# A recurrent attention and its MLP on one core: from 128-token chunks with bf16 parts to 64-token chunks in 64 by 64 tiles of TensorE

## The chip, the cores and the metric

The kernel runs on one core of one Trainium2 chip. TensorE (PE) multiplies matrices into PSUM, VectorE (DVE), ScalarE (ACT) and GpSimd (POOL) work on tiles in SBUF, SyncE (SP) issues every DMA. The metric is the time of one execution on the device in microseconds, as the median of the timed runs.

## The reference

For 4 batches and 8 heads a recurrence runs over 768 tokens; its output, 320 wide per token, goes through an MLP of width 2048 with a hard-swish between the layers. The numbers of a step are 40 wide.

```python
for t in range(S):                       # S = 768, D = 40
    m_new = np.maximum(f_gate[:, :, t] + m, i_gate[:, :, t])
    f_stab = np.exp(f_gate[:, :, t] + m - m_new)
    i_stab = np.exp(i_gate[:, :, t] - m_new)
    m = m_new
    C = f_stab[:, :, None, None] * C + i_stab[:, :, None, None] * np.einsum('bhd,bhe->bhde', vt, kt)
    n = f_stab[:, :, None] * n + i_stab[:, :, None] * kt
    h_tilde = np.einsum('bhde,bhe->bhd', C, qt)
    nq = np.einsum('bhd,bhd->bh', n, qt)[:, :, None]
    denom = np.maximum(np.abs(nq), 1.0)
    o = 1.0 / (1.0 + np.exp(-o_gate[:, :, t]))
    y[:, :, t] = o * h_tilde / denom
h = x @ w_in                             # x: y as (3072, 320); w_in (320, 2048), w_out (2048, 320)
g = h * np.clip(h + 3.0, 0.0, 6.0) / 6.0
out = g @ w_out
```

## The kernel before

**Units and tasks.** The 3072 tokens are eight units `u` of 384 (half of a batch). A unit has two tasks of four heads each (`quad`), and a task three chunks of 128 tokens (`cp`), so there are 48 chunks with four heads. The attention of unit u+1 is computed beside the MLP of unit u; the attention of unit 0 stands alone at the start, and unit 7's MLP alone at the end.

**A chunk.** The recurrence is worked in chunks: `gates` makes running sums of the gates for all heads; `gate` builds the tile `gw` of decays between the tokens of a chunk (load of the sums by all partitions, causal select on POOL, line 637, four exponentials on ACT, line 642). `front` multiplies q by k (`s`), then DVE multiplies by `gw`. `state` adds the chunk's sum of k and v (`c`) to the decayed state C. `back` multiplies by v and adds what C gives (`o`); `fin` divides, gates, transposes (`xa`, `xb`) and splits the result into `xh` and `xl`. Column 40 of v is 1, so that n is a column of C; two columns pad it to 42 (`E2`).

**Precision.** TensorE's fp32 matmul appears as two records in a profile. The first tasks (`QT` = 3, `PT` = 4) use it. Later ones split q, k, v, C and p into three bf16 parts (`load_qk`, `split_v`, the end of `state`, `front`) whose products are summed; the parts of q, k and C are stacked in 120 rows by further DMAs (`st<-spl`, `cS<-d`).

**The MLP.** `mm1` makes one of 16 tiles `h` with eight matmuls of 384 columns, ACT and DVE make `g` of it and split it into `gh` and `gl`; `mm2` adds three products per pair into three banks `acc` (in unit 0 plain fp32, line 918). `weight_slice` decodes 16 slices of the weights through ACT, DVE and POOL into `whi`, `wlo`, `wtl` and `vr`, line 818.

**The order.** Nothing is scheduled by the compiler. Each helper above is a job that yields an engine and a cost; the class `Plan` places all jobs by due times, costs and free buffers, and the program is recorded in that order. On the chip every engine takes its own queue in that order, and waits where an operand isn't there. `warm` fills places in which the plan has TensorE idle before the MLP starts with dummy matmuls `pw`. The numbers at the top of the file (due times, costs, letters in `ENGINES` that choose an engine) are the plan's inputs.

[...]

Of the kernel before, what the change touches and what calls it, by code (L numbers as in the profile page):

```python
# [17 lines left out]
L = 128  # L18
# [7 lines left out]
E2 = D + 2  # L26
WS = 8
WC = 640
NEG = -1.0e30
BIG = 3.0e38  # L30
NATW = U * 4 * (D + E2)
W_TINY = 2.0
W_HUGE = 65536.0 * 122880.0 - 512.0
QT = 3
PT = 4
GB = 2
# [3 lines left out]
SPAN = 50.047  # L40
T0 = 52.817
AH = 22.494
GP = [1, 1, 4]
G0 = -68.728
G1 = 0.617
AH1 = 34.491
FC = 1
FCS = [[(0, 3)], [(0, 2), (2, 1)], [(0, 1), (1, 1), (2, 1)], [(0, 1), (1, 2)]]
LON = 0.423
WAI = 32.907  # L50
WAO = 3.016
WAS = -8.005
MV = -3.516
DELTA = -0.043
EGW = 1
EV = 34.901
EG = 9.989
# [7 lines left out]
RATE = 3500  # L65
WN = 128
DELTA0 = 0.305
# [3 lines left out]
BL = 5.478  # L71
T_WARM = 6.9
STX = {0: "st", 1: "st", 2: "st", 7: "st", 8: "st", 9: "st", 10: "qk", 11: "spl"}
WGAP = 0.055
ENGINES = 'dppdddxddaadddddxdaaaaadaax'
BG = -0.135
BA = -0.976
BD = 1.378
GS = 6
FD = 2  # L80
FIN0 = 8.437
# [205 lines left out]
def mlstm_moe_kernel(ctx: ExitStack, tc: tile.TileContext, ig, fg, qkd, natd, ond, w_in, w_out, ident_d, out):  # L287
# [19 lines left out]
    cT = cst.tile([128, NC, BH], F32, name="cT")  # L307
    eG = cst.tile([128, NC, BH], F32, name="eG")
    wT = cst.tile([128, NC, BH], F32, name="wT")
    dec = cst.tile([D, NC, BH], F32, name="dec")  # L310
    gsc = dram.tile([NC, BH, L], F32, name="gsc")
    nc.vector.memset(half, 0.5)

    plan = Plan(dict(wm=1, s=1, o=1, cx=1, es=2, eo=1, ecx=1, qk=1, nat=1, vp=1, spl=1, vb=2, st=3, gw=3, p=2, ht=2, d=2, on=1, x=2,
                     egw=EGW, y=NY, raw=NRAW, mm=2, acc0=1, acc1=1, acc2=1, g=2, gs=GS, ob=3))
# [10 lines left out]

    def banks(u, tag):
        return (tag, "e" + tag) if u == 0 else (tag,)
# [20 lines left out]
    def warm():  # L349
# [12 lines left out]
        f_s=[BH, S], i_s=[BH, S], m_s=[BH, S], lf=[BH, S], g_s=[BH, S], last=[128, 128], gTs=[128, NC, BH], mask=[128, L], one=[BH, L], sel=[BH, 4, L]).items()}  # L362
# [6 lines left out]
    def gates(c0, n):  # L369
        f_s, i_s, m_s, lf, g_s, last, gTs, mask, one = (GT[k] for k in ("f_s", "i_s", "m_s", "lf", "g_s", "last", "gTs", "mask", "one"))  # L370
        if c0 == 0:
            yield "q", 200, 0.95
            nc.sync.dma_start(f_s, fg)
            nc.sync.dma_start(i_s, ig)
            nc.vector.memset(one, 1.0)
            nc.vector.memset(lf[:, 0:1], 0.0)
            if GB:
                sel = GT["sel"]
                nc.gpsimd.memset(sel, 1.0)
                nc.gpsimd.affine_select(sel, sel, pattern=[[-1, 4], [0, L]], compare_op=ALU.is_equal, fill=0.0, base=0, channel_multiplier=1)  # L380
                nc.gpsimd.memset(mask, BIG)
                nc.gpsimd.affine_select(mask, mask, pattern=[[1, L]], compare_op=ALU.is_ge, fill=NEG, base=0, channel_multiplier=-1)
# [12 lines left out]
        nc.vector.tensor_sub(lf[:, b:z], lf[:, b:z], m_s[:, b:z])  # L395
        for c in cs:
            ks = slice(c * L, c * L + L)
            yield "d", ld(L)
            nc.vector.tensor_tensor_scan(g_s[:, ks], one, lf[:, ks], 0.0, ALU.mult, ALU.add)
            event(f"g_s{c}")  # L400
# [3 lines left out]
        nc.sync.dma_start(gsc[hs].rearrange("c r t -> r c t"), g_s[:, a:z].rearrange("p (c t) -> p c t", c=n))  # L404
# [6 lines left out]
        gs = yield ("get",) + banks(0, "s")  # L411
        pc = bank(gs, [128, n, BH], f"pc{c0}")
        yield "p", mat(n, 128, 1, 32, 32)
        for c in cs:
            nc.tensor.transpose(pc[:, c - c0, :], i_s[:, c * L : (c + 1) * L], ident[:BH, :BH])
        go = yield ("get",) + banks(0, "o")
        pg = bank(go, [128, n, BH], f"pg{c0}")
        yield "p", mat(n, 128, 1, 32, 32)
        for c in cs:
            nc.tensor.transpose(pg[:, c - c0, :], g_s[:, c * L : (c + 1) * L], ident[:BH, :BH])  # L420
# [641 lines left out]
```

## Time and profile before

| what | value |
|---|---|
| timed runs | 585.59, 587.58, 589.38 us, median 587.58 |
| profiled execution, first to last instruction | 591.0 us (its time is given by this span alone) |
| busy: PE, DVE, ACT, POOL | 91%, 68%, 57%, 24% of the span |
| granted clock of TensorE, mean | 0.913 |
| DMA | 69.26 MB, 117 GB/s |
| stores of the eight units begin at | 174.9, 233.1, 298.3, 366.4, 423.7, 483.7, 540.6, 586.0 us |

[...] An engine's idle time is put down to what ended it.

### The profile page before, as it was taken

The numbers are of one execution on the slowest core, as the hardware profiler recorded it, in microseconds if no ns is written. First come the engines' busy times: TensorE is split into PE (matmuls) and PEld (weight loads), VectorE is DVE, ScalarE is ACT, GpSimd is POOL, SyncE is SP. The second block draws the span as 40 slices with busy tenths as digits, with TensorE's granted clock in tenths as the row PEclk, the third lists the DMA queues.
The fourth block names the chain that finished last, engine by engine and source line by source line (L and its number), as shares of the span: only waits on it lengthen the run. The fifth ranks groups of instructions, "written<-read, shape, count | busy, mean of one in ns | idle before, by whom it ended". The sixth has DMA issues, their size and how long they took to land.

```text
span 591.0 us, 11413 instructions
## 1 busy us (share of the span) xinstructions
PE 540.3 (91%) x4207; PEld 493.6 (84%) x4207; DVE 404.1 (68%) x849; ACT 337.8 (57%) x738; POOL 141.0 (24%) x191
## 2 busy tenths in 40 slices
PE   8999999687799897999789997999978998999997
PEld 7988899476679797889678896999868997999997
DVE  6443476997588767779767775796957677685433
ACT  4521164474746756667666666676756567544433
POOL 3242111543530312221211322132212203110000
PEclk9555588788999999999889998999989999999999
DMA  8524137549316226253454135344534244300000
GB/s 280 145 74 154 41 109 192 159 149 259 123 48 180 96 77 180 83 145 97 140 178 143 37 112 158 105 136 139 155 112 144 67 123 140 123 15 34 1 1 34
DMA packets 34548, 69.26 MB, mean 117 GB/s; under 512 B 4301, under 2 KB 14725, under 8 KB 34493
## 3 DMA queue, kind: packets, MB, share of 16 engines
q1 hardware_dynamic: 34493, 68.54, 38.0%
q8 instruction: 33, 0.54, 0.4%
q14 instruction: 22, 0.18, 0.1%
HBM read 42.66 MB, written 4.03 MB: 79 GB/s over the span
## 4 chain that ended last, share of the span: by engine, by line
PE 57%; DMA 16%; DVE 12%; ACT 7%; SPq 3%; issue 2%; POOL 1%; DVEq 0%; POOLq 0%; ACTq 0%
PE h L877 20%; DMA gw<-gsc 6%; PE acc L920 5%; PE acc L922 5%; PE acc L921 5%; PE pw L359 3%; DMA nat<-in_nat_dram 3%; PE o L701 3%; PE s L659 2%; DMA qk<-in_qk_dram 2%; PE c L581 2%; PE o L708 2%; PE s L662 2%; DMA rawi<-in_w_in_dram 2%; PE acc L918 2%
## 5 line engine op out<-in xcount | busy, mean ns | idle before, releaser
L877 PE MATMUL h<-xh,whi 128*128 128x384 f32 x256 | 95.4, 373 | 17.9 <-DVE g L893 17.8
L893 DVE SCALAR_TENSOR_TENSOR g<-g,h 128x384 f32<-128x384 f32 x128 | 70.1, 551 | 60.3 <-ACT g L891 59.7
L920 PE MATMUL acc<-vh,gh 128*128 128x320 f32 x336 | 108.6, 323 | 1.4 <-ACT gh L339 1.4
L891 ACT ACTIVATE g<-h,half 128x384 f32<-128x384 f32 x128 | 73.6, 576 | 57.4 <-PE h L877 49.7
L922 PE MATMUL acc<-vh,gl 128*128 128x320 f32 x336 | 104.1, 310 | 0.1
L921 PE MATMUL acc<-vl,gh 128*128 128x320 f32 x336 | 104.1, 310 | 0.0
L877 PE MATMUL h<-xl,whi 128*128 128x384 f32 x256 | 88.7, 347 | 0.0
L877 PE MATMUL h<-xh,wlo 128*128 128x384 f32 x256 | 88.7, 346 | 0.0
L642 ACT ACTIVATE gw<-gw,cT 128x128 f32<-128x128 f32 x192 | 65.4, 393 | 32.9 <-POOL gw L637 32.8
L637 POOL TENSOR_SCALAR_AFFINE_SELECT gw<-gw 128x512 f32<-128x512 f32 x46 | 33.2, 722 | 187.8 <-DMA gw<-gsc 144.1
L901 DVE TENSOR_TENSOR gl<-g,gh 128x384 fp32r<-128x384 f32 x112 | 63.8, 573 | 19.0 <-ACT gh L339 18.3
L339 ACT CAST gh<-g 128x384 fp32r<-128x384 f32 x112 | 57.1, 511 | 30.3 <-DVE g L893 29.5
L877 PEld LDWEIGHTS h<-xh,whi 128*128 128x128 f32 x256 | 50.2, 196 | 24.0 <-DVE g L893 23.1
L920 PEld LDWEIGHTS acc<-vh,gh 128*128 128x128 f32 x336 | 63.6, 189 | 2.2 <-ACT gh L339 1.9
L922 PEld LDWEIGHTS acc<-vh,gl 128*128 128x128 f32 x336 | 63.4, 189 | 0.6 <-DVE gl L901 0.6
L921 PEld LDWEIGHTS acc<-vl,gh 128*128 128x128 f32 x336 | 63.7, 190 | 0.0
L339 ACT CAST p<-gw 128x512 bf16<-128x512 f32 x72 | 44.2, 614 | 19.7 <-DVE gw L666 13.8
L877 PEld LDWEIGHTS h<-xl,whi 128*128 128x128 f32 x256 | 50.3, 196 | 0.2
L877 PEld LDWEIGHTS h<-xh,wlo 128*128 128x128 f32 x256 | 50.2, 196 | 0.0
L877 PE MATMUL h<-xl,wtl 128*128 128x384 f32 x128 | 45.0, 352 | 0.4 <-DVE xl L784 0.3
L877 PE MATMUL h<-xh,wtl 128*128 128x384 f32 x128 | 44.5, 348 | 0.0
L666 DVE TENSOR_TENSOR gw<-s,gw 128x512 f32<-128x512 f32 x48 | 33.0, 687 | 16.7 <-PE s L662 9.5
(118 smaller groups left out, 1096.8 us busy)
## 6 DMA issues: line engine op xcount, KB each, us to landing
st<-spl SPq DMA_DIRECT2D x117, 160.0 KB
gw<-gsc SPq DMA_DIRECT2D x46, 256.0 KB
nat<-in_nat_dram SPq DMA_DIRECT2D x16, 492.0 KB
qk<-in_qk_dram SPq DMA_DIRECT2D x13, 480.0 KB
rawi<-in_w_in_dram SPq DMA_DIRECT2D x8, 640.0 KB
rawo<-in_w_out_dram SPq DMA_DIRECT2D x8, 640.0 KB
on<-in_on_dram SPq DMA_DIRECT2D x8, 480.0 KB
out_dram<-ob SPq DMA_DIRECT2D x24, 160.0 KB
```

Of the source, the lines that this page charges most:

```text
L339: nc.scalar.copy(dst, src)
L359: nc.tensor.matmul(pw[:, :WN], ones[:, :128], ones[:, :WN], start=True, stop=True)
L637: nc.gpsimd.affine_select(gw, gw, pattern=[[0, 4], [1, L]], compare_op=ALU.is_ge, fill=NEG, base=0, channel_multiplier=-1)
L642: nc.scalar.activation(gw[:, h, :], gw[:, h, :], AF.Exp, bias=cT[:, c, r0 + h : r0 + h + 1], scale=1.0)
L666: nc.vector.tensor_tensor(gw, sp, gw, ALU.mult)
L877: nc.tensor.matmul(hp, w, x, start=n == 0, stop=n == len(seq) - 1)
L891: nc.scalar.activation(g, hp, AF.Relu, bias=half, scale=1.0 / 6.0)
L893: nc.vector.scalar_tensor_tensor(g, g, 1.0, hp, ALU.min, ALU.mult)
L901: E(e).tensor_sub(gl, g, gh.bitcast(F32))
L920: nc.tensor.matmul(acc, gh[:, ts_], VH[f // 4][:, f % 4, :], start=f == 0, stop=False)
L921: nc.tensor.matmul(acc, gh[:, ts_], VL[p][:, f % 2, :], start=False, stop=False)
L922: nc.tensor.matmul(acc, gl[:, ts_], VH[f // 4][:, f % 4, :], start=False, stop=f == NF - 1)
```

## The change

Chunks are 64 tokens long, and two of them are worked together, so that a step still covers 128 tokens and four heads. Everything in attention is plain fp32; the bf16 parts, their casts and subtractions and their stacking DMAs are gone. The four 64 by 64 tiles of the array work on different heads or chunks: a matmul names its tile by the partitions of its operands (0 to 63 or 64 to 127) and of its output. One TensorE group writes one PSUM tile `xy` of two banks and holds B (the output) of the step before, S (q by k) and K (the state) of this one, 32 matmuls; in unit 0 S and K are one group and B another. `gate` works on 256 columns: the causal mask and the key's gate are added by DVE and one exponential follows. A task loads its gate sums at once. The state C is 128 partitions wide and steps twice per group. The heads of a unit are laid out in another order, and the rows of `w_in` with them. The cast for `vh` goes to DVE, the tail sums for `wtl` to POOL. The buffers are `st` 2, `nat` 2, `gw` 3 per task; before `nat`, `vp`, `qk` and `spl` had one each, `st` and `gw` three per chunk. The plan's inputs differ throughout; one line of them stands in the diff.

```diff
-ENGINES = 'dppdddxddaadddddxdaaaaadaax'
+ENGINES = 'dyxpxppdydaxdyyyzdaxxyadayydd'
-    plan = Plan(dict(wm=1, s=1, o=1, cx=1, es=2, eo=1, ecx=1, qk=1, nat=1, vp=1, spl=1, vb=2, st=3, gw=3, p=2, ht=2, d=2, on=1, x=2,
+    plan = Plan(dict(wm=1, xy=1, exy=1, z=1, es=1, eo=1, st=2, nat=2, gw=NGW, ht=2, on=1, x=2,
...
 def gate(task, cp):
...
+        else:
+            whole = task > 1
+            if not whole or cp == 0:
+                yield "wait", f"gsc{part * U + U - 1 if whole else c}"
+                lo, n = (part * U * L, U) if whole else (c * L, 1)
+                t0 = plan.now["t"]
+                for h in range(2):
+                    plan.now["t"] = t0
+                    yield "q", 66 * n
+                    r = 16 * h + 2 * bq
+                    nc.sync.dma_start((gt if whole else gw)[h * Q : h * Q + Q].rearrange("p j c t -> p j (c t)"), gsc[r : r + 2, lo : lo + n * L].partition_broadcast(Q))
+                event(f"gl{nm}")
+            elif whole:
+                yield "wait", f"gl{task}_0"
+            e = yield pick(27, g=0.72, d=ld(256))
+            E(e).tensor_tensor(gw, gw, mask[:, None, None, :].broadcast_to([128, 2, 2, Q]), ALU.add)
+        yield "wait", f"cT{c}"
+        e = yield pick(28, g=0.64, d=ld(256))
+        E(e).tensor_tensor(gw, gw, cT[:, 2 * c : 2 * c + 2, 2 * bq : 2 * bq + 2].rearrange("p c j -> p j c")[:, :, :, None].broadcast_to([128, 2, 2, Q]), ALU.add)
+        yield "a", ca(256) + 0.08
+        nc.scalar.activation(gw, gw, AF.Exp)
...
+    def group(g, parts):
+        u = parts[0][1] // (2 * U)
+        got = yield ("get", "xy", "exy") if u == 0 and g < GE else ("get", "xy")
+        pool = early["ps"] if got[0] == "exy" else ps_at
+        xy = pool.tile([128, 2, 512], F32, tag=f"{got[0]}{got[1]}", name=f"xy{g}")
...
+        for kind, n in parts:
+            task, cp = divmod(n, U)
...
+            if kind == "S":
+                st = T["st"][0]
+                for j in range(2):
+                    for c in range(2):
+                        rs = slice(c * Q, c * Q + D)
+                        for h in range(2):
+                            nc.tensor.matmul(xy[h * Q : h * Q + Q, c, j * Q : j * Q + Q], st[rs, cp, j, h], st[rs, cp, j, 2 + (h != c)], start=True, stop=True)
+            elif kind == "K":
+                for j in range(2):
+                    for c in range(2 if ch < NC - 1 else 1):
+                        rs = slice(c * Q, c * Q + Q)
+                        for h in range(2):
+                            o = (cp * 4 + 2 * h + j) * D
+                            nc.tensor.matmul(xy[h * Q : h * Q + KM, c, 296 + j * E2 : 296 + j * E2 + E2], T["kn"][rs, o : o + KM], T["vn"][rs, cp, 2 * h + j], start=True, stop=True)
+            else:
+                st, gt, vh = T["st"][0], T["gw"][0], T["vh"]
+                C0 = Cs.get((b, quad, ch - 1, 1), zero)
+                C1 = Cs[(b, quad, ch, 0)]
+                for j in range(2):
+                    for h in range(2):
+                        rs = slice(h * Q, h * Q + D)
+                        for c in range(2):
+                            nc.tensor.matmul(xy[c * Q : c * Q + Q, h, 212 + j * E2 : 212 + j * E2 + E2], st[rs, cp, j, 2 if c == h else 4], (C1 if c else C0)[rs, j], start=True, stop=True)
+                for j in range(2):
+                    for h in range(2):
+                        rs = slice(h * Q, h * Q + Q)
+                        for c in range(2):
+                            nc.tensor.matmul(xy[c * Q : c * Q + Q, h, 128 + j * E2 : 128 + j * E2 + E2], gt[rs, j, 2 * cp + c], vh[rs, cp, c, j], start=True, stop=True)
...
 def front(task, cp):
...
+        yield "d", cd(256)
+        nc.vector.tensor_tensor(gw, xy[:, :, 0:128].rearrange("p c (j t) -> p j c t", j=2), gw, ALU.mult)
...
 def state(task, cp):
...
+            Cn = at.tile([128, 2, E2], F32, tag=f"C{quad}", name=f"C{nm}_{c}", bufs=6)
+            if cur is None:
+                e = yield pick(8, a=ca(84), d=cd(84))
+                cast(e, Cn[:R], kv[:R, c])
+            else:
+                e = yield psub(16, 84)
+                E(e).tensor_tensor(Cn[:R], cur[:R], dec[:R, ch, c, 2 * bq : 2 * bq + 2, None].broadcast_to([R, 2, E2]), ALU.mult)
+                yield "d", cd(84)
+                nc.vector.tensor_add(Cn[:R], Cn[:R], kv[:R, c])
...
 def back(task, cp):
...
+        nc.vector.tensor_tensor(hv, xy[:, :, 212:296].rearrange("p h (j e) -> p h j e", j=2), heads(eG[:, c], bq)[:, :, :, None].broadcast_to([128, 2, 2, E2]), ALU.mult)
+        yield "d", cd(168)
+        nc.vector.tensor_add(hv, hv, xy[:, :, 128:212].rearrange("p h (j e) -> p h j e", j=2))
```

Three places of the order show the change. The first is TensorE in the middle of unit 2's MLP (`h2`): before, `c` of a chunk of task 7 stands there, followed by its `o`, of which the first matmuls are shown (`p`, `vb`, `st`, `cS` are bf16 parts).

```order
L877 MATMUL h2_11_3090<-xl2_1903,wtl_77 128x384
L581 MATMUL c7_1_3075<-vp7_2879,nat7_2841 40x42 x4
L703 LDWEIGHTS p7_1_2942
L703 MATMUL o7_1_3118<-vb7_2880,p7_1_2942 128x84
L704 LDWEIGHTS p7_1_2942
L704 MATMUL o7_1_3118<-vb7_2880,p7_1_2942 128x42
L705 LDWEIGHTS p7_1_2942
L705 MATMUL o7_1_3118<-vb7_2880,p7_1_2942 128x84
L706 LDWEIGHTS p7_1_2942
L706 MATMUL o7_1_3118<-vb7_2880,p7_1_2942 128x42
```

Now the last B of task 6 (`xy21`, by `st` and C, then by `gw` and `nat`) stands with S (`st` alone) and K of the first step of task 7 behind a piece of `h2`; the next piece of `h2` follows.

```order
L826 MATMUL h2_1_2746<-xl2_2092,wtl_77 128x384
L626 MATMUL xy21_2698<-C6_1_1_2620,st6_2063 64x42
L626 MATMUL xy21_2698<-C6_2_0_2677,st6_2063 64x42
L626 MATMUL xy21_2698<-C6_1_1_2620,st6_2063 64x42
L626 MATMUL xy21_2698<-C6_2_0_2677,st6_2063 64x42
L626 MATMUL xy21_2698<-C6_1_1_2620,st6_2063 64x42
L626 MATMUL xy21_2698<-C6_2_0_2677,st6_2063 64x42
L626 MATMUL xy21_2698<-C6_1_1_2620,st6_2063 64x42
L626 MATMUL xy21_2698<-C6_2_0_2677,st6_2063 64x42
L631 MATMUL xy21_2698<-nat6_2064,gw6_1709 64x42 x8
L610 MATMUL xy21_2698<-st7_2454 64x64 x8
L617 MATMUL xy21_2698<-nat7_2455 64x42 x8
```

What was three separate pieces among `h` and `acc` is one piece. The second place is TensorE in the cold start, before any `h`: before, the second chunk of task 0 has its `c` and its `o`, on 128 columns of weights, with the next `c` behind.

```order
L581 MATMUL c0_1_461<-vp0_143,nat0_106 40x42 x4
L701 MATMUL o0_1_462<-nat0_106,gw0_1_114 128x42
L708 MATMUL o0_1_462<-C0_0_450,st0_1_148 128x42
L701 MATMUL o0_1_462<-nat0_106,gw0_1_114 128x42
L708 MATMUL o0_1_462<-C0_0_450,st0_1_148 128x42
L701 MATMUL o0_1_462<-nat0_106,gw0_1_114 128x42
L708 MATMUL o0_1_462<-C0_0_450,st0_1_148 128x42
L701 MATMUL o0_1_462<-nat0_106,gw0_1_114 128x42
L708 MATMUL o0_1_462<-C0_0_450,st0_1_148 128x42
L581 MATMUL c0_2_494<-vp0_143,nat0_106 40x42 x4
```

Now S and K of the second step (`xy1`) and B of the first (`xy100`) stand there, in tiles of 64; `zero` is the empty state.

```order
L610 MATMUL xy1_425<-st0_110 64x64 x8
L617 MATMUL xy1_425<-nat0_111 64x42 x8
L626 MATMUL xy100_457<-zero_82,st0_110 64x42
L626 MATMUL xy100_457<-C0_0_0_421,st0_110 64x42
L626 MATMUL xy100_457<-zero_82,st0_110 64x42
L626 MATMUL xy100_457<-C0_0_0_421,st0_110 64x42
L626 MATMUL xy100_457<-zero_82,st0_110 64x42
L626 MATMUL xy100_457<-C0_0_0_421,st0_110 64x42
L626 MATMUL xy100_457<-zero_82,st0_110 64x42
L626 MATMUL xy100_457<-C0_0_0_421,st0_110 64x42
L631 MATMUL xy100_457<-nat0_111,gw0_109 64x42 x8
L451 MATMUL pl2_480<-gTs_102,last_101 128x128
```

The number of `pw` ahead of the first `h` goes from 277 to 411. The third place is POOL while the last weight slices (`vr`) are made: before, it has the select on `gw`, `vb`, `d` and C among them.

```order
L637 AFFINE_SELECT gw4_2_1384<-gw4_2_1384 128x512
L637 AFFINE_SELECT gw5_0_1493<-gw5_0_1493 128x512
L565 TENSOR_TENSOR vb4_1420<-nat4_1402,vb4_1420 128x12x42
L604 TENSOR_TENSOR d4_0_1543<-dr4_0_1544,d4_0_1543 40x168
L818 TENSOR_TENSOR vr5_1599<-yo5_1425,rawo5_1392 128x640
L818 TENSOR_TENSOR vr6_1650<-yo6_1477,rawo6_1457 128x640
L588 TENSOR_TENSOR C4_1_1657<-C4_0_1536,dec_84 40x168
L637 AFFINE_SELECT gw5_1_1646<-gw5_1_1646 128x512
L818 TENSOR_TENSOR vr7_1715<-yo7_1538,rawo7_1514 128x640
```

Now only half-wide steps of C and the products of v with the gates (`nat`, in place) stand among them.

```order
L665 TENSOR_TENSOR C4_1_0_1825<-C4_0_1_1729,dec_86 128x84
L767 TENSOR_TENSOR vr6_1873<-yo6_1752,rawo6_1718 128x640
L665 TENSOR_TENSOR C4_1_1_1879<-C4_1_0_1825,dec_86 128x84
L527 TENSOR_TENSOR nat5_1708<-nat5_1708,wT_85 128x168
L767 TENSOR_TENSOR vr7_1911<-yo7_1831,rawo7_1789 128x640
L527 TENSOR_TENSOR nat5_1708<-nat5_1708,wT_85 128x168 x2
L665 TENSOR_TENSOR C4_2_0_1980<-C4_1_1_1879,dec_86 128x84
L665 TENSOR_TENSOR C4_2_1_2002<-C4_2_0_1980,dec_86 128x84
L665 TENSOR_TENSOR C5_0_1_2085<-C5_0_0_2062,dec_86 128x84
```

The select on `gw`, which followed a load, is no longer in POOL's queue.

More of the change, by code (lines that the diff above doesn't have):

```diff
@@ L522, in load_on @@
+        event(f"vh{task}")
     def load_on(u):
@@ L530, in load_on, with heads @@
         event(f"on{u}")
+    def heads(x, bq):
+        return x.rearrange("p (h q j) -> p h q j", h=2, q=NB)[:, :, bq]
     def weigh(task):
[L533 to L540 removed]
+        u, quad, b, part, bq = where(task)
+        vn = tasks[task]["vn"]
+        for cp in range(U):
+            c = part * U + cp
+            yield "wait", f"wT{c}"
@@ L684, in back @@
     def back(task, cp):
-        u, quad, b, part, r0 = where(task)
+        u, quad, b, part, bq = where(task)
         T = tasks[task]
```

585 lines of the change are left out of this document (238 added, 347 removed).

## The prediction

> **What bounds the kernel now.** I read the stages first, then the chain and the waits inside each. One query cuts the span at the first MoE matmul (85 us) and at the eight stores of `ob` that end a unit (175, 236 and so on). The columns are length, then busy time and instructions of each engine, granted clock of TensorE, DMA share, GB/s.
>
> ```profile
> core 0: us, PE busy (x) PEld busy (x) DVE busy (x) ACT busy (x) POOL busy (x), PEclk, DMA share, GB/s
> 12.00:73.00 61.00, 59.97 (x358) 52.77 (x356) 26.87 (x67) 19.38 (x53) 17.77 (x25) 0.50 0.39 116
> 73.00:85.00 12.00, 12.00 (x112) 10.73 (x110) 9.78 (x28) 8.66 (x20) 0.68 (x1) 0.93 0.23 76
> 85.00:175.00 90.00, 76.17 (x427) 62.71 (x427) 68.12 (x132) 49.11 (x100) 39.40 (x34) 0.86 0.53 157
> 175.00:236.00 61.00, 55.60 (x453) 50.97 (x452) 46.97 (x93) 40.79 (x90) 11.12 (x19) 1.00 0.45 133
> 236.00:299.00 63.00, 55.90 (x529) 52.01 (x528) 49.74 (x103) 43.21 (x94) 14.51 (x23) 0.97 0.41 124
> 299.00:366.00 67.00, 58.31 (x476) 54.58 (x476) 46.27 (x93) 42.36 (x95) 15.84 (x22) 0.96 0.39 119
> 366.00:424.00 58.00, 57.03 (x528) 53.94 (x527) 45.90 (x99) 40.13 (x91) 15.78 (x23) 0.99 0.42 125
> 424.00:485.00 61.00, 54.65 (x472) 51.22 (x470) 43.70 (x93) 39.08 (x90) 11.31 (x18) 0.97 0.37 116
> 485.00:541.00 56.00, 53.55 (x485) 50.55 (x483) 40.08 (x89) 32.77 (x69) 10.30 (x16) 1.00 0.27 86
> 541.00:591.00 50.00, 46.61 (x287) 44.64 (x285) 19.20 (x36) 18.79 (x38) 0.00 (x0) 1.00 0.06 20
> ```
>
> TensorE is the nearest to full in every stage, but each stage has its own limit. From 12 to 73 us it is busy 59.97 of 61 us at half its clock: the start is a TensorE queue running cold. Unit 0 (85 to 175) has 13.8 us of idle TensorE and a clock of 0.86. Units 1 to 6 take 366 us, of which TensorE is busy 335 (the sum of six rows) and idle 31. Unit 7 has no attention beside it.
>
> What fills the cold start is in the groups of that stretch (line, operation, count, then busy us and mean ns):
>
> ```profile
> L359 PE MATMUL pw<-ones 128*128 128x128 bf16 x157 | 19.1, 312 | 0.0
> L701 PE MATMUL o<-nat,gw 128*128 128x42 f32 x48 | 14.1, 423 | 1.0 <-DVE gw L666 1.0
> L659 PE MATMUL s<-st 40*128 40x128 f32 x48 | 12.4, 438 | 0.0
> L708 PE MATMUL o<-C,st 40*128 40x42 f32 x32 | 10.4, 425 | 0.0
> L581 PE MATMUL c<-vp,nat 128*40 128x42 f32 x56 | 5.5, 277 | 0.0
> ```
>
> So 42 us are fp32 attention on 128-wide weights, 19 us the dummy matmuls `pw`. When the clock comes back is told by a piece of the chain (start, length) and two stretches:
>
> ```profile
> 69.05 3.85 PE pw L359 x35
> ...
> 69.80:73.20 3.40, 3.40 (x33) 3.40 (x31) 1.20 (x2) 0.00 (x0) 1.44 (x2) 0.50 0.03 5
> 73.20:76.00 2.80, 2.80 (x32) 2.38 (x30) 2.10 (x10) 2.64 (x7) 0.00 (x0) 0.99 0.00 0
> ```
>
> 35 `pw` in a row, 110 ns each, are followed by the full clock.
>
> In the middle, rows of the timeline (start, busy, line, count) give what attention costs TensorE, from one start to the next:
>
> ```profile
> 255.30 0.21 PE L703 MATMUL o<-vb,p 128*128 128x84 bf16 x1
> ...
> 255.97 0.20 PE L711 MATMUL o<-cS,st 120*128 120x42 bf16 x2
> 256.02 0.40 PE L920 MATMUL acc<-vh,gh 128*128 128x320 f32 x1
> 256.26 0.31 PE L921 MATMUL acc<-vl,gh 128*128 128x320 f32 x1
> 256.40 0.31 PE L922 MATMUL acc<-vh,gl 128*128 128x320 f32 x1
> ...
> 256.99 0.62 PE L662 MATMUL s<-st 120*128 120x128 bf16 x8
> 257.42 0.39 PE L920 MATMUL acc<-vh,gh 128*128 128x320 f32 x1
> ...
> 261.82 0.50 PE L581 MATMUL c<-vp,nat 128*40 128x42 f32 x8
> 262.26 0.41 PE L920 MATMUL acc<-vh,gh 128*128 128x320 f32 x1
> ...
> 265.35 1.39 PE h L877 x8
> ```
>
> `o` takes 0.72 us (255.30 to 256.02), `s` 0.43, `c` 0.44. That is 1.59 us per chunk of 128 tokens and four heads. The first `acc` after each change of shape holds its slot 0.24 us, the next ones 0.146 ((256.99 - 256.26) / 5): each change costs 0.1 us, three to a chunk. The MoE itself needs 16 x 1.39 = 22.2 us for `h` and 144 x 0.146 = 21.0 for `acc`: 43.2 per unit.
>
> The idle 31 us of units 1 to 6 end on these waits (us in total, times, longest):
>
> ```profile
> PE h L877 <- DVE g L893: 11.8, 9, 2.7
> PE c L581 <- POOL vp L542: 7.0, 4, 3.5
> PE xa L766 <- DVE C L341: 3.8, 1, 3.8
> ...
> POOL gw L637 <- DMA gw<-gsc: 121.5, 24, 9.8
> ```
>
> The last row is why: in-order POOL sits at the head of its queue for a gate load that arrives late, and `vp`, `d` and C behind it come late to TensorE; DVE's `g` queues behind the splitting of `p` and `qk`.
>
> **The change, part by part.** *Vector engines.* The bf16 parts go, and four exponentials per chunk become one:
>
> ```profile
> L642 ACT ACTIVATE gw<-gw,cT 128x128 f32<-128x128 f32 x192 | 65.4, 393 | 32.9 <-POOL gw L637 32.8
> ...
> L339 ACT CAST p<-gw 128x512 bf16<-128x512 f32 x72 | 44.2, 614 | 19.7 <-DVE gw L666 13.8
> ...
> L673 DVE TENSOR_TENSOR gw<-gw,p 128x512 f32<-128x512 f32 x36 | 26.0, 723 | 10.3 <-ACT p L339 10.1
> ```
>
> On ACT 144 exponentials (57 us by the 393 ns) and 44 us of casts vanish, beside smaller ones. On DVE this row's 26 us go, with a sister of the same size and the subtractions on `qk`, `nat` and `C`, while 90 new 256-wide additions on the gate come (by half the 723 ns, some 33 us, since the row's tile is 512 wide) and 48 C steps become 80 half-wide ones. None of this was on the path by itself; it empties the queues ahead of `g`. The POOL select on `gw` goes to DVE, so POOL no longer stands before a gate load; loads come one per task into two or three buffers where `nat` had one. Two waits are new: group n holds B of chunk n-1, so TensorE waits in it for `front` (one DVE multiplication, 0.4 us by the same halving) and for C; and one PSUM slot `xy` must be emptied between groups. Behind a late group stands all MoE work, but about 7 us of it lies between two groups (49 us over 7). I therefore leave 10 us of the 31 idle us in units 1 to 6 (ends: 4 and 31).
>
> *TensorE, per group.* 32 fp32 matmuls are 64 records, if they pair as `c` does (8 records for 4). No row of before packs tiles, so bounds: `c` takes 55 ns per record for 40 weight columns, and
>
> ```profile
> 119.00 0.40 PE L701 MATMUL o<-nat,gw 128*128 128x42 f32 x2
> 119.23 0.22 PE L711 MATMUL o<-cS,st 120*128 120x42 bf16 x2
> ```
>
> 115 ns for 128; at 64 columns that is 71 ns, so 4.5 us if nothing overlaps, 2.3 if two tiles do, 1.1 if all four do. The closest starts anywhere are 25 ns (`L711` above: two in 0.05 us), giving 1.6 us. I take **1.6**, nearest to that row, plus 0.2 for the changes of shape, with 1.1 and 4.5 as ends. Before, a chunk cost 1.59 + 0.3. So in the middle the packing alone is worth nothing to speak of; what counts is the idle time.
>
> [...]
>
> *Start.* Up to the first `h` the order has 411 `pw` (277 before) and 9.5 chunks (about 9 before). Of the 277, 157 lie between 12 and 73 us (row above) and some 46 after, so 74 in the first 12 us; if that stays, 337 are left. At full clock one `pw` takes 72 ns, by a row from before the cold stretch:
>
> ```profile
> 9.97 0.79 PE L359 MATMUL pw<-ones 128*128 128x128 bf16 x11
> ```
>
> Then 337 are 24 us, chunks 9.5 x 1.8 = 17, transposes and gate matmuls 6: the first `h` at 59. Cold: 156 `pw` by 110 ns (17), the run of 54 (6), six chunks at twice 1.8 (22), the small ones 10: 67 us; after 54 in a row the clock returns, as after 35 above, and 127 `pw` (9) with 3.5 chunks (6) and transposes (1) follow: 83. I take **70**, about the middle. The cover here is that TensorE, not the chain, limits; were it the chain, 85 would stay.
>
> *Unit 0* holds eight pieces of fp32 `acc` like this one from the chain:
>
> ```profile
> 168.61 3.32 PE acc L918 x12
> ```
>
> Its work is 22.2 us of `h`, 26.6 of `acc`, four chunks (7.2) and transposes 1.4: 57 us. Before, five chunks lay here at fp32 prices, and clock and idle together took the rest. I leave 9 us for the clock (0.86 cost 12.6) and the idle 14, which is the weight pipeline: **80** (ends 70 and 105, where weights arrive as late as before).
>
> *Units 1 to 6.* 6 x 43.2 = 259 for MoE, 35 groups x 1.8 = 63, transposes and their changes 9, idle 10, cold 4: **345**, against 366. Unit 7: 50 as now.
>
> Sum: 70 + 80 + 345 + 50 = 545 for the span, against 591. The timed runs' median, 587.58, is 3.4 under that span; so **542**.
>
> **Rivals.**
> *Weights hold unit 0.* Its end stays at 175 whatever attention does: 175 + 345 + 50 - 3.4 = 567. For it: slices pass through ACT, DVE and POOL and unit 0 idles 13.8 us; against: DVE, 68 of 90 us busy there, is relieved.
> [...]
> *Slower: no packing.* At 4.5 us per record chain, 2.9 x 39 + 28 or more: above 680. It decides from (587 - 542) / (39 + 13) = 0.86 us over my 1.6, that is 2.46 us per group. Against it: nothing but the four tiles' separate rows and columns; for it: 55 ns per record with one tile in use.
> *All goes well.* Group 1.1, first `h` at 59, unit 0 in 70, idle 4: 59 + 70 + 322 + 50 - 3.4 = 498.
> *The change does not do what it says* can be left out: the order shows the groups.
>
> **How the numbers follow.** Forecast 0.60 (525 to 560), weights 0.14, pairs 0.10, no packing 0.08, all well 0.08. A range of 508 to 584 leaves out most of the last two, about 0.16, and some of the pairs. A measurement of this kernel tells about 1% from no change. Faster by over 1% (under 581.7): the forecast, weights, all well and under half of the pairs, 0.85; within 1%: 0.06; slower: 0.09.
>
> **What would show it.** A group's span, from its first start to the next `h` or `acc`: under 2 us, or the pairs or none. The first `h` before 80 us, with PEclk above 0.5 before it. The last `vr` add on POOL before 165 us, or weights hold unit 0. TensorE's idle in the six middle units: 10 us, not 31, with waits on `gw<-gsc` gone from POOL. I am wrong if a new wait of a group on `front`, C or `xy` takes more than 1 us each time, or if the array's low activity in the groups costs clock windows: each of 3.4 us at half clock is 1.7.

## The result, and the profile after

The changed kernel takes 521.64 us (median of 4 runs, 518.08 to 525.46), against 586.59 for the kernel before on the same chip: a ratio of 0.894, with a 95% interval of 0.887 to 0.901. The prediction was 542, range 508 to 584. The profiled execution has a span of 516.4 us. The ratio counts only executions in the faster of two states (before: 581.89 and 585.59), and the two profiled executions lie at opposite ends, 516.4 the shortest of the changed kernel and 591.0 longer than every timed run before, so some 10 of the 75 us by which they differ are not the change's.

The head of its page, the clock by fortieths, then the stages (cut at the first `h` and at the stores of `ob` after unit 0 and after unit 6; columns as in the prediction):

```profile
span 516.4 us, 13614 instructions
...
PE 481.1 (93%) x5805; PEld 448.4 (87%) x5805; DVE 318.2 (62%) x809; ACT 205.0 (40%) x406; POOL 89.8 (17%) x171
...
PEclk9658998999999999999989899989999999999999
```
```profile
12.00:68.00 56.00, 51.16 (x1089) 46.44 (x1087) 38.44 (x119) 18.50 (x44) 21.82 (x37) 0.76 0.62 172
68.00:136.00 68.00, 58.19 (x554) 46.67 (x546) 53.68 (x118) 31.63 (x56) 31.94 (x37) 0.97 0.54 153
136.00:469.00 333.00, 318.42 (x3782) 304.00 (x3783) 200.84 (x515) 135.88 (x272) 33.88 (x86) 0.98 0.27 70
469.00:516.00 47.00, 44.11 (x274) 42.86 (x272) 17.60 (x34) 17.51 (x35) 0.00 (x0) 1.00 0.06 22
```

The first `h` starts at 68 instead of 85 us (-17), unit 0 takes 68 instead of 90 (-22), units 1 to 6 take 333 instead of 366 (-33), unit 7 takes 47 instead of 50 (-3). Together 75 us of the span, where the medians lie 65 apart; in which stage the 10 us too many stand, these two profiles do not tell. In units 1 to 6 TensorE's idle is halved, from 31 us to 14.6, and its busy time falls by 16.6.

That second half comes from the groups. One group in the timeline of TensorE (start, busy, line):

```profile
203.50 0.44 PE L626 MATMUL xy<-C,st 40*64 40x42 f32 x16
203.75 0.42 PE L631 MATMUL xy<-nat,gw 64*64 64x42 f32 x16
203.98 0.44 PE L610 MATMUL xy<-st 40*64 40x64 f32 x16
204.24 0.40 PE L617 MATMUL xy<-nat 64*64 64x42 f32 x16
204.57 0.44 PE L826 MATMUL h<-xh,whi 128*128 128x384 f32 x1
204.85 0.34 PE L826 MATMUL h<-xl,whi 128*128 128x384 f32 x1
```

Rows overlap (the second one starts 0.25 us after a first that is busy 0.44), so a cost is the step from start to start. The first `h` behind the group's 64 records starts 1.07 us after the first of them: **1.07 us** for a group, 16.7 ns a record, where before one chunk took 1.59 us in bf16 parts. Behind it the first `h` holds its slot for 0.28 us instead of 0.17: one change of shape costs 0.1 us.

The waits of TensorE and then of VectorE between 136 and 469 us (total, times, longest) show what is left of the idle (an arrow points from the waiting line to what it waits for):

```profile
PE acc L871 <- DVE gl L850: 11.9, 6, 2.2
PE xa L727 <- DVE on L716: 0.9, 2, 0.7
PE xy L626 <- DVE C L667: 0.8, 1, 0.8
...
DVE gw L569 <- DMA gw<-gsc: 19.0, 7, 3.4
```

The waits that the groups themselves add (`xy` for C or for `front`) are almost nothing. The large one is `acc` for `gl`, a step of the MLP (the prediction's MoE) that the change does not touch. The timeline says why (SyncE issues the load, VectorE waits for it, TensorE waits for VectorE):

```profile
249.84 1.23 SPq L564 DMA_DIRECT2D gw<-gsc  x2
...
259.34 0.42 DVE L569 TENSOR_TENSOR gw<-gw,mask 128x256 f32<-128x256 f32 x1 [3.24 <-DMA gw<-gsc]
259.68 0.55 DVE L850 TENSOR_TENSOR gl<-g,gh 128x384 fp32r<-128x384 f32 x1
...
260.29 0.41 PE L871 MATMUL acc<-vh,gl 128*128 128x320 f32 x1 [2.20 <-DVE gl L850]
...
298.12 0.41 DVE L645 TENSOR_TENSOR gw<-xy,gw 128x256 f32<-128x256 f32 x1
```

The load is queued behind 1.3 MB of `st` and `nat` and lands some 9 us after its issue. VectorE stands 3.24 us at the mask addition for it; `gl`, which is ready, stands behind; TensorE loses 2.2 us. Yet these gates belong to the task after the one whose `st` was loaded with them (task 11, by the order of the 48 multiplications), and their first use is the multiplication at 298.12, 39 us later.

The stops also cost clock. In units 1 to 6 there are four stretches of 3.4 us at half clock, from 179.6, 261.6, 285.5 and 336.7 us on. Each begins 2.3 to 3.5 us after the start of a stop of 2.07 to 2.23 us at `gl`; the two shorter stops at `gl`, 1.74 and 1.51 us, have none behind them. One of the four:

```profile
261.60:265.00 3.40, 3.40 (x13) 3.40 (x13) 2.49 (x9) 0.75 (x2) 0.77 (x2) 0.50 0.00 0
```

Half of 3.4 us is lost each time, 6.8 us in all.

### The profile page after: what moved, and what is told of

Read it like the earlier page. It is cut to its first block, busy times and chain, and to the rows that moved or that the text cites. A ratio compares the mean times of both kernels' runs of the same rounds, so it can differ in the third digit from the quotient of the medians.

```text
span 516.4 us, 13614 instructions
## 1 busy us (share of the span) xinstructions
PE 481.1 (93%) x5805; PEld 448.4 (87%) x5805; DVE 318.2 (62%) x809; ACT 205.0 (40%) x406; POOL 89.8 (17%) x171
## 4 chain that ended last, share of the span: by engine, by line
PE 55%; DMA 21%; DVE 15%; ACT 3%; POOL 2%; issue 2%; SPq 1%; ACTq 0%; POOLq 0%; DVEq 0%
PE h L826 22%; DMA gw<-gsc 11%; PE acc L871 8%; PE acc L869 7%; PE acc L870 7%; DMA rawo<-in_w_out_dram 4%; PE pw L371 3%; DMA nat<-in_nat_dram 3%; DMA rawi<-in_w_in_dram 3%; DVE g L842 2%; DVE gw L569 2%; DVE gw L572 2%; DVE gl L850 2%; PE xy L626 1%; ACT g L840 1%
## 5 line engine op out<-in xcount | busy, mean ns | idle before, releaser
L871 PE MATMUL acc<-vh,gl 128*128 128x320 f32 x336 | 106.5, 317 | 11.9 <-DVE gl L850 11.9
L869 PE MATMUL acc<-vh,gh 128*128 128x320 f32 x336 | 106.0, 316 | 0.3 <-ACT gh L351 0.3
L826 PE MATMUL h<-xh,wlo 128*128 128x384 f32 x256 | 86.5, 338 | 0.7 <-DVE wlo L785 0.7
L826 PE MATMUL h<-xl,whi 128*128 128x384 f32 x256 | 86.7, 339 | 0.0
L665 POOL TENSOR_TENSOR C<-C,dec 128x84 f32<-128x84 f32 x80 | 31.0, 391 | 188.7 <-DVE C L667 137.3
L826 PEld LDWEIGHTS h<-xh,wlo 128*128 128x128 f32 x256 | 48.7, 190 | 1.0 <-DVE wlo L785 1.0
L826 PE MATMUL h<-xl,wtl 128*128 128x384 f32 x128 | 43.3, 338 | 0.0
L574 ACT ACTIVATE gw<-gw 128x256 f32<-128x256 f32 x48 | 19.5, 417 | 52.4 <-DVE gw L572 52.3
L371 PE MATMUL pw<-ones 128*128 128x128 bf16 x411 | 35.3, 256 | 3.6 <-issue 2.5
L527 POOL TENSOR_TENSOR nat<-nat,wT 128x168 f32<-128x168 f32 x48 | 23.5, 511 | 81.7 <-DMA nat<-in_nat_dram 53.1
```

The costliest lines, as they stand in the source:

```text
L371: nc.tensor.matmul(pw[:, :WN], ones[:, :128], ones[:, :WN], start=True, stop=True)
L527: E(e).tensor_tensor(v, v, heads(wT[:, c], bq)[:, :, :, None].broadcast_to([128, 2, 2, E2]), ALU.mult)
L574: nc.scalar.activation(gw, gw, AF.Exp)
L665: E(e).tensor_tensor(Cn[:R], cur[:R], dec[:R, ch, c, 2 * bq : 2 * bq + 2, None].broadcast_to([R, 2, E2]), ALU.mult)
L826: nc.tensor.matmul(hp, w, x, start=n == 0, stop=n == len(seq) - 1)
L869: nc.tensor.matmul(acc, gh[:, ts_], VH[f // 4][:, f % 4, :], start=f == 0, stop=False)
```

## The experiments

Theory P: the packing makes the group cheap. Theory V: the vector work that went was the brake. Theory D: the 22 MB of transfers that went were. Theory G, from the rows above: the late gate load at the head of VectorE's queue costs what is still to be had. The expectations also name S: a new plan only moves the waits about, and what it wins is a lucky order. All kernels below but one are the changed kernel with one edit; line numbers shift by a few. The runs were made on several chips, with the kernel before beside them, which took 581.5 to 586.6 us there (medians); a difference of under 1%, some 6 us, to the changed kernel is therefore not clear of noise, and the ratio to the kernel before is the surer measure. This table has the median and, from one profiled execution each, the stages (us; unit 0 and units 1 to 6 as lengths, idle of TensorE in units 1 to 6):

| kernel | median | first h | unit 0 | units 1-6 | idle |
|---|---|---|---|---|---|
| before | 586.6 | 85.0 | 89.9 | 365.7 | 31.0 |
| changed | 521.6 | 68.0 | 67.8 | 332.9 | 14.6 |
| serial | 608.1 | 82.9 | 68.8 | 409.5 | 0.8 |
| unpacked | 659.8 | 75.3 | 100.1 | 433.3 | 0.4 |
| vec | 573.4 | 71.3 | 77.6 | 374.4 | 47.4 |
| vecact | 548.8 | 66.6 | 81.2 | 351.1 | 29.0 |
| dma | 557.6 | 72.4 | 72.8 | 361.2 | 32.6 |
| dmabehind | 525.5 | 73.1 | 73.3 | 334.1 | 14.6 |
| gdelay8 | 494.9 | 58.8 | 73.2 | 312.3 | 1.4 |
| gpool | 514.8 | 68.9 | 69.7 | 325.6 | 9.0 |
| gdelayt6 | 497.2 | 68.1 | 68.4 | 310.2 | 0.3 |
| rate240 | 490.2 | 64.9 | 62.5 | 311.6 | 0.3 |
| pairrow | 539.9 | 74.3 | 67.1 | 349.1 | 10.0 |
| paircol | 534.2 | 67.3 | 70.2 | 347.3 | 8.9 |

### serial: the four tiles one after another

```diff
-    nc.tensor.matmul(xy[...], ...)        # round the four tiles
+    mm(row, col, xy[...], ...)            # order.append((row, col, args)), then:
...
+        for row, col, args in sorted(order, key=lambda o: o[:2]):
+            nc.tensor.matmul(*args, start=True, stop=True)
```

> The changed kernel with the same matmuls, emitted tile by tile inside each group (all of the group's matmuls of one 64 by 64 tile, then the next tile's) instead of going round the four tiles. Nothing else moves. Theory P (the groups are cheap because four tiles work at once): a group's 64 records no longer overlap and take about 55 ns each, as the 42-column fp32 records of the kernel before did in c (0.44 us for 8), so 3 to 3.5 us instead of 1.07; with 35 groups beside the MoE in units 1 to 6 and TensorE 96% busy there, about 75 to 85 us more in units 1 to 6, about 600 to 620 us in all. Rival I (the 16.7 ns per record are the pace at which TensorE issues, whatever the tiles, and the gain came with fewer changes of shape): a group stays within 0.2 us of 1.07 and the time within 5 us of 522.

Measured 608.12 us (603.33 to 610.65), ratio to before 1.040 (1.032 to 1.049). The timeline of one group, first records, last ones and the `h` behind:

```profile
259.31 0.42 PE L644 MATMUL xy<-C,st 40*64 40x42 f32 x4
259.57 0.40 PE L644 MATMUL xy<-nat,gw 64*64 64x42 f32 x4
...
262.32 0.37 PE L644 MATMUL xy<-nat 64*64 64x42 f32 x4
262.63 0.69 PE L833 MATMUL h<-xh,whi 128*128 128x384 f32 x1
```

And units 1 to 6 as one stretch, with the 3.4 us behind this group below it:

```profile
151.70:561.20 409.50, 408.70 (x3833) 396.58 (x3830) 203.37 (x515) 136.47 (x272) 33.98 (x86) 0.93 0.22 57
262.60:266.00 3.40, 3.40 (x13) 3.37 (x12) 2.10 (x8) 0.58 (x2) 0.33 (x1) 0.50 0.67 177
```

The same matmuls in another order take 3.32 us a group, and 52 ns per record over units 1 to 6. P holds: the cheap group is the four tiles at work together. The other order costs 77 us in units 1 to 6, 15 in the start, 1 in unit 0. So most of the start's 17 us hangs on the packing (its groups take 33 us of TensorE there instead of 14, from start to start), and unit 0's 22 us do not.

The first row holds a second price: TensorE is busy 408.70 of 409.50 us, yet the clock is 0.93, below the 0.98 of the changed kernel, which idles 14.6 us. There are 15 stretches at half clock in it, and each begins 2.2 to 3.8 us after a group's first start, about where the group ends, as in the second row. `unpacked` below has no small tiles and idles 0.4 us, and it too has 15 such stretches and 0.94. So the lower clock goes with long pieces of the small fp32 matmuls of attention, in tiles or not; the reason is not shown.

### unpacked: the kernel before in plain fp32

```diff
-QT = 3
-PT = 4
+QT = 16
+PT = 16
```

(beside it, two `nat` buffers, and the `st` slots for all later chunks)

> The kernel before with the bf16 parts taken out but nothing packed: all 16 tasks use the fp32 matmuls on the full array that its first tasks used (chunks of 128 tokens), q/k are loaded as they are, no split of p, v or the state; two nat buffers so that the release after the last o stalls nothing. Theory P+V (TensorE's cheap group and the relief of the vector engines and queues are both needed): s, c and o cost 2.4 to 3.4 us of TensorE per chunk instead of 1.59, which over the 36 chunks that used bf16 adds 30 to 65 us, against at most 31 us of idle TensorE in units 1 to 6 to win: 595 to 630 us, slower than before. Rival V (the gain is the vector work and transfers that went, packing is beside the point): the idle TensorE of units 1 to 6 goes from 31 to about 15 us and the time falls to 560 to 575 us.

Measured 659.75 us (658.81 to 677.55), ratio 1.129 (1.120 to 1.138). Slower than the 630 expected at most: `s` alone takes 1.09 us to the next start (it was 0.43 in bf16):

```profile
301.08 1.16 PE L659 MATMUL s<-st 40*128 40x128 f32 x8
302.17 0.42 PE L920 MATMUL acc<-vh,gh 128*128 128x320 f32 x1
```

Over units 1 to 6 `s`, `c` and `o` cost 127 us for 33 chunks, 3.85 us each, against 1.59 in bf16 parts and 1.07 packed. The idle of TensorE vanishes (0.4 us), and nothing is gained by it. Dropping the bf16 parts without packing loses 73 us; V alone is refuted.

### vec and vecact: the vector work put back

```diff
 def front(task, cp):
     ...
     done(g)
     ...
+    if task > 1:
+        for _ in range(3):
+            nc.vector.tensor_tensor(sd, sd, sd, ALU.add)   # not in vecact
+        for _ in range(5):
+            nc.scalar.copy(sa, sa)
```

> The changed kernel with about the removed vector work put back as work that nothing reads: after the multiplication of the gates of each chunk from task 2 on, three additions of 128x512 on VectorE (some 0.6 us each, 76 us in all) and five copies of 128x512 on ScalarE (some 0.53 us each, 111 us in all), outside the chain of the attention but in the queues of both engines. Theory P+V: half of what units 1 to 6 won (16 us) was waits on these queues, so the time rises by 12 to 25 us, to 534 to 547, and the idle of TensorE in units 1 to 6 returns to 25 to 35 us. Rival P alone (only the TensorE time counts): within 5 us of 522. Rival V: most of the 65 us come back, 560 or more.

Measured 573.38 us (572.06 to 574.16), ratio 0.982 (0.974 to 0.989): 52 us slower than the changed kernel; in the profiled execution 3 in the start, 10 in unit 0, 41 in units 1 to 6. Over the whole of it VectorE and ScalarE are busy 409 and 327 us, before the change 404 and 338. The 52 us are the number that V gave, almost three times the middle of what P with V gave. The waits of TensorE between 149 and 523 us:

```profile
PE acc L880 <- DVE gl L859: 24.4, 24, 2.0
PE xy L630 <- DVE C L676: 18.7, 9, 3.8
PE xa L736 <- DVE on L725: 2.0, 3, 0.9
```

`gl` is late four times as often as after the change, and C, whose additions now stand behind three long ones, is late too. These additions do not stand exactly where the removed ones stood, so 52 us is a price of this load at this place, not of the removed work to the microsecond.

> The idle work put back on ScalarE alone: five copies of 128x512 per chunk from task 2 on (0.62 us each in the run with both, 105 us), none on VectorE. If the 52 us of that run came from VectorE's queue (theory G: VectorE is the engine at which gl, C and p queue), this one costs 10 to 20 us: 532 to 542. If they came from ScalarE (the relu between h and the gates of the MoE is late behind the copies), 550 to 570.

Measured 548.84 us (546.75 to 551.28), ratio 0.946 (0.939 to 0.953): 27 us, between the two theories. ScalarE's load alone costs half of what both cost. In unit 0 it is worse than both engines loaded (81 us against 78), and POOL's last `vr` begins at 140.84, 74 us after the first `h`; after the change it is 62 us (130.51), before 85 (170.32):

```profile
140.84 1.55 POOL L774 TENSOR_TENSOR vr<-yo,rawo 128x640 uint32<-128x640 uint32 x1 [0.82 <-issue]
```

So a good part of unit 0's 22 us hangs on ScalarE's queue. Every weight slice passes through it, but that the weights are what comes late is not shown: TensorE idles 15.4 us in this unit 0 and waits, between 66.6 and 148 us, mostly for `g` and `xh`, the MLP's own steps (11.5 us), and less for the weights `wlo` and `vr` (3.1):

```profile
PE h L833 <- DVE g L849: 4.0, 2, 2.4
PE h L833 <- ACT xh L738: 3.8, 1, 3.8
PE acc L874 <- DVE g L849: 3.7, 2, 2.5
PE h L833 <- DVE wlo L792: 2.3, 1, 2.3
PE acc L874 <- POOL vr L774: 0.8, 1, 0.8
```

### dma and dmabehind: the bytes put back

```diff
 def load_nat(task):
...
         event(f"nat{task}")
+        nc.sync.dma_start(junk[task][0].rearrange("u d w -> d u w"), qkd[task].rearrange("u d w -> d u w"))
+        nc.sync.dma_start(junk[task][1], natd[task])
...
         nc.sync.dma_start(nat[:, KW + VW :], natd[task, :, KW + VW :])
```

In `dmabehind` the two new lines stand behind the gate loads of tasks 2 to 15.

> The changed kernel with the removed bytes put back: with each load of nat, the task's whole q/k and nat blocks are also copied from DRAM to a place in DRAM that nothing reads, 22 MB in all, the difference between the two kernels. Theory P+V (in the start TensorE in its cold queue ends last, in the middle only the gate loads wait for transfers): the gate loads land some 5 us later and VectorE stands longer at them, 5 to 15 us more, 527 to 537; the first h stays within 4 us of 68. Rival D (the transfers' relief is most of the gain of start and unit 0, 39 us): first h at 75 to 85 us and the first unit's end at 160 or later, 555 or more. Rival P alone: within 3 us of 522.

Measured 557.60 us (555.82 to 558.06), ratio 0.954 (0.948 to 0.960): 36 us, the number that D gave, but not in D's places: the first `h` is only 4 us later and unit 0 ends at 145. 28 us lie in units 1 to 6, at the gate load (profiled execution). TensorE and VectorE between 145 and 506 us:

```profile
PE acc L875 <- DVE gl L854: 27.6, 6, 5.5
...
DVE gw L573 <- DMA gw<-gsc: 41.9, 8, 6.6
```

> The copies of q/k and nat from DRAM to DRAM once more, 1.38 MB per task in tasks 2 to 15, but issued right behind the task's gate load instead of ahead of it (it copies nothing in tasks 0 and 1). Theory G: not the bytes cost the 36 us of the run with the copies in front, but their place ahead of the gate load; behind it the acc wait for gl stays near 12 us and the time is 524 to 532. Rival D (the transfers take the time whatever their place, by the rate of the shared queues): 545 to 560.

Measured 525.49 us (523.22 to 529.97), ratio 0.906 (0.898 to 0.915). Behind the gate load 19 MB instead of 22 cost 4 us by the medians, 7 by the ratios, and the two waits stay where they were:

```profile
PE acc L876 <- DVE gl L855: 11.2, 6, 2.1
...
DVE gw L574 <- DMA gw<-gsc: 19.0, 8, 3.2
```

What costs 28 us in units 1 to 6 in the one and 1 us in the other is not the amount but the place in the queue, ahead of a load for which VectorE waits. There D is refuted, and G gains. In the start and unit 0 both profiled executions are 9 to 11 us longer than the changed kernel's, which the two runs leave open.

### gdelay8, gpool, gdelayt6: the gate load

```diff
 nc.sync.dma_start(gw, gsc...)         # shortened
+plan.now["t"] += 8.0 * whole          # gdelayt6: * (task >= 6)
 event(f"gl{nm}")
```

> The changed kernel with one line more: from task 2 on, the planner takes the gate load of a task as landed 8 us later than it did, so it lets VectorE go on with other work before the mask addition that waits for that load. The load itself and what needs it (a task later) stay. Theory G (VectorE stands at the head of its queue for a load that nobody needs yet, and TensorE waits for the gl behind it; each such stop also lets the clock fall for a window of 3.4 us): the 19.0 us of VectorE at the gate load in units 1 to 6 fall under 3, the 11.9 us of acc for gl under 4, idle TensorE from 14.6 to 5, the cold windows at 261 and 285 us go: 8 to 16 us less, 506 to 514. Rival S (the orders of the engines are tuned to each other and any new plan loses elsewhere what it wins): within 4 us of 522, with the wait at another line.

Measured 494.90 us (492.08 to 498.23), ratio 0.853 (0.847 to 0.859), better than expected by 11 to 19 us. Idle TensorE in units 1 to 6 is 1.4 us, the wait for the gate load is gone. But the start is 9 us shorter too, and unit 0 5 us longer, where the planner's order had changed.

> The changed kernel with the mask addition of the gates of tasks 2 to 15 on GpSimd instead of VectorE: the same wait for the gate load at the head of another queue. Theory G: acc no longer waits for gl (11.9 us fall under 4), but GpSimd now stands for the load, and behind it the products for the new state, C, which xy waits for; the wait moves to xy for C at 3 to 10 us, time 512 to 522. Rival S: as without the edit or slower, 520 to 530, because the addition on GpSimd is about twice as long and its orders shift.

Here the mask addition is GpSimd's (`ENGINES[27]` from `d` to `p`). Measured 514.82 us (512.33 to 516.06), ratio 0.887 (0.879 to 0.895). That the addition is about twice as long on GpSimd was the author's estimate; the trace of the changed kernel has multiplications of 128x168, 511 ns on GpSimd and 325 on VectorE. As expected the wait moves to `xy`, and 7 us are won instead of 27, in units 1 to 6 of the profiled execution as in the median. By the ratios (0.887 and 0.894, overlapping intervals) these 7 us are not clear of noise, so that the time alone does not decide against S. TensorE between 139 and 464 us:

```profile
PE xy L626 <- DVE C L667: 4.9, 5, 2.1
PE acc L871 <- DVE gl L850: 1.8, 4, 0.8
PE acc L869 <- ACT gh L351: 1.2, 3, 0.6
```

> The 8 us of delay for the gate load only from task 6 on (unit 3), so that every engine's order in the start and in unit 0 stays that of the changed kernel. In the run with the delay from task 2 on, 21 of the 27 us were won in units 1 to 6 and 9 in the start, where the order had changed too. Theory G: only units 1 to 6 gain, through the wait itself: first h stays at 68, the end of unit 0 at 136, and units 1 to 6 win 12 to 18 us of those 21 (the waits of task 4 and 5 stay): 503 to 510. Rival S (what the first run won was a lucky order, not the wait): 517 to 524 with TensorE idle 10 us or more in units 1 to 6.

Measured 497.24 us (495.96 to 499.77), ratio 0.857 (0.853 to 0.862). TensorE's order in the start and in unit 0 is that of the changed kernel, and both stages take what they took there, 68.1 and 68.4. Units 1 to 6 alone win 23 us:

```profile
136.50:446.70 310.20, 309.87 (x3799) 297.68 (x3789) 200.93 (x516) 135.24 (x272) 34.84 (x86) 1.00 0.30 75
```

14.3 of them are idle, the other 8.4 shorter steps: with no stop left, the clock is 1.00 where it was 0.98; the four stretches at half clock that are gone were 6.8 of them. The wait for the gate load no longer appears in VectorE's list, and `gdelay8`, with another order up to unit 0, has the same 310 to 312 us in units 1 to 6. This is G; S is refuted for the middle. It is more than the 12 to 18 us expected, since no stop hung on the gates of tasks 4 and 5, which kept the old plan: the first of the seven in the changed kernel belongs to task 8.

### rate240: every transfer planned at 240 GB/s

```diff
-self.dma = max(self.dma, self.free[e] + DMA0) + cost / 360.0
+self.dma = max(self.dma, self.free[e] + DMA0) + cost / 240.0
```

> The changed kernel whose planner counts every transfer at 240 GB/s instead of 360 (240 is near what the stretches with long transfers moved, 226 to 269 GB/s in the slices of 200 to 330 us), with no delay for the gate load alone. Theory G: it plans the gate loads, among all others, some 2 to 4 us later, which covers a part of the lateness (the loads landed up to 3.4 us after VectorE stood at them): idle TensorE in units 1 to 6 falls under 8 us and the time to 500 to 515. Rival S: a new order of everything, start and unit 0 above all, loses 5 us or more there: 520 to 530.

Measured 490.18 us (488.84 to 497.26), ratio 0.844 (0.840 to 0.848), the fastest version here: 31 us under the changed kernel. Its stages:

```profile
12.00:64.90 52.90, 49.41 (x1107) 45.23 (x1105) 40.11 (x119) 18.94 (x44) 25.23 (x39) 0.87 0.66 185
64.90:127.40 62.50, 58.59 (x610) 47.88 (x611) 57.09 (x122) 32.41 (x56) 31.08 (x37) 0.97 0.57 168
127.40:439.00 311.60, 311.34 (x3788) 298.70 (x3788) 202.10 (x513) 134.34 (x270) 34.84 (x85) 1.00 0.29 75
```

The middle gains as with the delay for the one load (311.6). Start and unit 0 gain 8 us more; no run here separates what the other order and what the shorter waits do there.

### pairrow and paircol: two tiles by turns

The order of `serial`, but going by turns between two tiles that share their rows (`pairrow`) or their columns (`paircol`).

> The changed kernel with each group's matmuls going by turns between two tiles that share their rows (row group, the contraction side) and differ in their columns, first for the upper rows, then for the lower. Nothing else moves. If tiles overlap only when their row groups differ, a group costs what it cost tile by tile, some 50 ns per record, 3.2 us; if any two tiles overlap, 25 ns per record, 1.6 to 1.8 us, and the time is 540 to 550.

> The changed kernel with each group's matmuls going by turns between two tiles that share their columns (the output side) and differ in their row group, first for the left columns, then for the right. If only different row groups overlap, 25 ns per record, 1.6 to 1.8 us a group and 540 to 550 in all, while the run with shared rows stays near 608; if any two tiles overlap, the two runs are alike.

One run each: 539.91 and 534.19 us. A group in the timeline of each, `pairrow` first, from its first record to the next `h`:

```profile
258.64 0.43 PE L648 MATMUL xy<-C,st 40*64 40x42 f32 x8
...
260.46 0.45 PE L837 MATMUL h<-xh,whi 128*128 128x384 f32 x1
```
```profile
254.97 0.43 PE L648 MATMUL xy<-C,st 40*64 40x42 f32 x8
...
256.79 0.45 PE L837 MATMUL h<-xh,whi 128*128 128x384 f32 x1
```

1.82 us both times; over units 1 to 6, 28.5 and 29.1 ns per record. Two tiles of the same rows overlap like two of the same columns; two that share neither were not run.

## Why the prediction was right, and where it was off

The sign and the main mechanisms held, and 521.6 lies in the range; the sum was 20 us too high. Against the span it was 545 for 516: 12 us too many in unit 0, 12 in units 1 to 6, 5 elsewhere. The profiled execution now lies 5 us under the median, before 3.4 above it, so that the correction had the wrong sign.

*Group: mis-sized.* 1.6 us was taken, from the closest starts on full tiles (25 ns); 1.07 was measured, the lower end of the bounds. That "in the middle the packing alone is worth nothing to speak of" fails: attention takes 36 us of TensorE in units 1 to 6 where it took 52, and with 0.1 us for the change of shape in place of 0.2, some 20 us of the forecast's 63 for groups were too many. The 1.1 us that came true is the bound from the prediction's own rows, four tiles at work at once (71 ns, an estimate, divided by four). In the trace packed tiles start some 7 ns apart only within a round of four (39.57, 39.58, 39.59, 39.59 us in one group); the next record follows 0.03 us later (39.62), and over a group the mean is 16.7. No run shows the 2.3 us of the pairs, to which the prediction gave 0.10: with two tiles by turns a group took 1.82, in `pairrow` as in `paircol`.

*Start: right, in part by luck.* 70 said, 68.0 measured, with the clock at 0.76. 70 was taken about midway between 59 and 83 for want of a way to tell how long the clock stays low. From start to start the groups took 14.1 us there, where the two ends had 17 and 28, and 4.8 us of idle that neither end had made up for part of it. That TensorE limits there is shown by `serial`: the same start with dearer groups ends 15 us later. Single profiled executions differ there by some us, though: `pairrow` and `paircol`, with equally dear groups, end it at 74.3 and 67.3.

*Unit 0: too long.* 80 was said with an end of 70; it took 67.8. The 57 us of work were right (58.19 busy). What failed is the 9 us left for the clock and the 14 for idle: the clock is 0.97, which costs 1.7 us, and idle is 10. `vecact` and `vec` give back 13 and 10 us of the 22, as idle (15.4 and 13.4 us) and as clock (0.90 and 0.89), and `serial` 1. So the relief of the vector engines' queues, costed at nothing there, was about half. The prediction called all 14 us of idle the weight pipeline; by the waits only a part of it was, 5.3 us for `vr` before (1.8 after the change) beside 5.9 for `g`. The rival that weights hold unit 0 at 175 us is refuted (135.8), with the last `vr` at 130.5, well before the 165 named.

*Idle in units 1 to 6: nearly right in size, wrong in cause.* 10 us said, 14.6 measured. New waits in the groups stay under 1 us there, as said, and half-clock stretches follow stops, not groups. But "POOL no longer stands before a gate load" was half a sentence: VectorE stands there now, ahead of `gl`. Stops also cost more beyond themselves than thought: 14.6 us of idle went with 8 us of slower steps, as `gdelayt6` shows, where 4 were left for the clock. These 9 us too few covered part of the 20 too many for groups, so that the 345 for units 1 to 6 came out nearer (333) than its terms. And vector work is dearer than thought: `vec` brings 33 us of idle back where 10 to 20 were expected.

*Unit 7:* 47, 50 said.

So the 65 us came from two sides that needed each other: without packing, plain fp32 loses 73 us; with packing but about the old load on the vector engines most of the gain, 52 of 65 us, is gone. The buffers, the one gate load per task and the other inputs of the plan were not tested apart. A further 31 us lay in the plan: 21 of them in units 1 to 6, where a later landing of the gate load alone wins as much; what wins the rest in the start and unit 0 is open.

## What to carry to other kernels

Here the small fp32 matmuls on a packed array paid only because consecutive matmuls went to different tiles (522 us; 608 tile by tile); check the order of emission before anything else. When a step moves to another engine, ask what now waits at that engine's queue head, and for which transfer: a load needed 39 us later cost 24 us here because an in-order engine stood for it. Check a planner's transfer times against the trace: later landings in the plan (240 GB/s in place of 360) were worth 31 us, nearly half as much as the whole change.

## What the hardware showed that was not expected

- A record of a 64 by 64 fp32 tile costs 52 ns when its tile works alone, 29 with two and 17 with four; two that share rows cost what two that share columns cost.
- A TensorE that is never idle can be granted less clock than one that stops: 0.93 in units 1 to 6 of `serial` (0.8 us of idle) and 0.94 of `unpacked` (0.4), against 0.98 with 14.6 us of idle. In `serial` every stretch at half clock begins about where a group of attention ends.
- Stops of about 2 us on TensorE cost more than their length, through the clock: four stops of 2.07 to 2.23 us were each followed by 3.4 us at half clock. No threshold is shown: stops of 1.51 and 1.74 us were not, one of 1.72 us in `paircol` was. 14.3 us of idle and 8.4 of slower steps went together.
- Nineteen MB of additional transfers cost 4 us (7 by the ratios) behind the load that an engine waits for, and 22 MB cost 36 ahead of it.
